# The output product of pairs 1 to 3 as seven half-size products, and a written-out order for every engine

## The chip, the cores and the metric

The kernel runs on one core of one Trainium2 chip. The metric is the device time of one execution in microseconds, given as the median of the timed runs; lower is better.

## The reference, cut to what matters

Attention in two stages (32 packed queries `p` attend to `k`, `v`; then the 576 queries `q` attend to the packed result) gives `x` of 4608 tokens by 512. A feed-forward layer follows, and it is most of the work:

```python
p_packed = sm_attn(p, k, v)
out = sm_attn(q, p_packed, p_packed)          # 8 batches, 8 heads, 576 queries, 64 wide
x = out.transpose(0, 2, 1, 3).reshape(4608, 512)
h = x @ w_in                                   # 512 -> 2048
g = 0.5 * h * (1.0 + erf(h / sqrt(2)))
return (g @ w_out).astype(np.float32)          # 2048 -> 512
```

Everything is float32.

## The kernel before, in words

The eight batches are worked in four pairs (`pr` 0 to 3), and the 2048 hidden columns in four blocks of 512 (`f`), so there are 16 units `u = 4 * pr + f`. In pair 0 the weights come from DRAM, are decoded to full words on ACT, DVE and POOL (`decode`), and are kept in a DRAM scratch (`keep`); pairs 1 to 3 load them from there, one 512 KB piece at a time (`w<-ws`, L1774).

Float32 accuracy is had from three matmuls in the rounded type float32r: each operand is split into a high part (a cast on ACT) and a low part (operand minus high part, on DVE), and high x high, high x low and low x high are added up in PSUM.

A unit has eight hidden steps (`hidden_steps`, L1936 to L1974): a step gives 128 hidden columns of one batch, 12 matmuls of 288 columns on L1957 into a `wide` tile (two buffers of two PSUM banks). `gelu` (L1976) takes it through Gelu on ACT (L1979), then splits it: 512 of the 576 tokens on ACT (L1986) and DVE (L1988) into `g`, the other 64 on POOL (L1999, L2000) into `t4`, the tile of the tokens at the edge of both batches. Each hidden step is followed by an output step (`output_steps`, L2034): four token tiles of 128, three matmuls of 512 columns each (`three`, L2008: L2009, L2010, L2011), with a token tile of `g` as the weights and a row block of `w_out` as the moving operand. Four output steps fill a PSUM tile; `edge_output` does the same for the edge tile. `finish` (L2111) copies the PSUM tile into `acc` at `f = 0` (L2115, ACT), adds it at later `f` (L2120, DVE), and writes the rows out at `f = 3`. The very last edge tile is done in two halves of 256 columns (`last_rows`, L2083; L2101, L2102).

The order of the instructions on each engine is fixed at build time. `Order` plays the kernel as a set of tasks against modelled costs (the second argument of each `Op`) and at each turn of an engine issues the first ready operation by a priority, made of the tables `SLACK`, `EARLY` and `SOONER` and of `PATIENCE`. The attention of pair `pr + 1` runs on all engines beside the units of pair `pr`. All DMAs are issued by SP's queue, in order.

## Time and profile before

| what | value |
|---|---|
| timed runs | 721.12 us median of 3 (720.46 to 721.38) |
| profiled execution | span 718.7 us, first to last instruction; what lies around the span isn't in the page, and the timed runs are 1.8 to 2.7 us above it |
| granted TensorE clock | mean 1.000 of full |
| busy | PE 99%, weight loads 82%, DVE 54%, ACT 49%, POOL 23% |
| DMA | 106.76 MB, 149 GB/s mean |

A PE instruction's time in the profile is from its start to its modelled end, and the next one starts before that end; so a rate is read from the starts of a run of matmuls, and not from their durations.

### The profile page before, as it was taken

To read this page: it belongs to the slowest core of one execution; us is meant where nothing else is said; L and a number is where in the kernel's file an instruction comes from. 1 tells how busy PE (TensorE), PEld (TensorE's weight loads), DVE (VectorE), ACT (ScalarE), POOL (GpSimd) and SP (SyncE) were. 2 spreads that over 40 slices of the span, in tenths; PEclk is the share of its full clock that TensorE was granted. 3 is DMA by queue.
4 is the path that set the end of the run, shared out by engine and by line. 5 is a ranking of instruction groups with operands and counts; after the bars stand their busy time and mean duration, and the time that the engine had idled before them with its cause. 6 is when DMAs were issued, how large, how long until landed. Compare 5 with 4: busy or idle time off the path is not lost.

```text
span 718.7 us, 13236 instructions
## 1 busy us (share of the span) xinstructions
PE 712.2 (99%) x5278; PEld 586.0 (82%) x5278; DVE 389.5 (54%) x613; ACT 350.9 (49%) x589; POOL 162.1 (23%) x318
## 2 busy tenths in 40 slices
...
GB/s 320 355 212 222 210 260 184 225 203 298 135 102 156 179 180 188 8 225 18 163 81 146 228 172 209 9 110 75 131 158 42 222 60 88 60 29 88 1 118 73
DMA packets 156797, 106.76 MB, mean 149 GB/s; under 512 B 124353, under 2 KB 132801, under 8 KB 156737
## 3 DMA queue, kind: packets, MB, share of 16 engines
...
## 4 chain that ended last, share of the span: by engine, by line
PE 94%; DMA 2%; DVE 2%; ACT 1%; SPq 0%; issue 0%; ACTq 0%
PE h L1957 26%; PE o L2009 17%; PE o L2011 16%; PE o L2010 16%; PE wps L1891 4%; PE h L1948 2%; PE s L1351 2%; PE o_edge L2009 2%; PE o_edge L2011 2%; PE o_edge L2010 2%; PE pp L1544 1%; DMA wraw<-in_moe_w_in_dram 1%; PE idle L1930 1%; DMA v<-in_v_dram 1%; PE e1Tm L1457 1%; DVE wp L1907 1%
## 5 line engine op out<-in xcount | busy, mean ns | idle before, releaser
L1957 PEld LDWEIGHTS h<-a2T,wp 128*128 128x128 f32 x1440 | 202.9, 188 | 9.8 <-PE h L1957 0.5
L1957 PE MATMUL h<-a2T,wp 128*128 128x288 f32 x1440 | 210.2, 295 | 0.3 <-DVE wp L1907 0.3
L2009 PE MATMUL o<-w,g 128*128 128x512 f32 x508 | 204.1, 402 | 0.0
L2011 PE MATMUL o<-w,g 128*128 128x512 f32 x508 | 198.5, 391 | 0.2 <-DVE g L1988 0.2
L2010 PE MATMUL o<-w,g 128*128 128x512 f32 x508 | 198.4, 391 | 0.0
L1988 DVE TENSOR_TENSOR g<-graw,g 128x512 fp32r<-128x512 f32 x128 | 93.3, 731 | 182.8 <-ACT g L1986 179.9
L1979 ACT ACTIVATE graw<-h 128x576 f32<-128x576 f32 x128 | 83.3, 652 | 200.2 <-PE h L1957 151.4
L1999 POOL CAST t<-graw 128x64 fp32r<-128x64 f32 x128 | 39.8, 311 | 466.7 <-ACT graw L1979 283.5
L2009 PEld LDWEIGHTS o<-w,g 128*128 128x128 f32 x508 | 95.4, 188 | 37.0 <-issue 21.5
L2011 PEld LDWEIGHTS o<-w,g 128*128 128x128 f32 x508 | 95.4, 188 | 21.8 <-DVE g L1988 0.6
L2010 PEld LDWEIGHTS o<-w,g 128*128 128x128 f32 x508 | 95.4, 188 | 14.9
L1986 ACT CAST g<-graw 128x512 fp32r<-128x512 f32 x128 | 79.4, 621 | 56.2 <-PE o L2011 53.7
L2120 DVE TENSOR_TENSOR acc<-o,acc 128x512 f32<-128x512 f32 x96 | 63.5, 684 | 36.2 <-PE o L2011 36.1
L1907 DVE TENSOR_TENSOR wp<-wps,wp 128x1024 fp32r<-128x1024 f32 x30 | 35.9, 1218 | 29.6 <-ACT wp L1902 29.5
L2000 POOL TENSOR_TENSOR t<-graw,t 128x64 fp32r<-128x64 f32 x128 | 46.9, 366 | 10.2
L1902 ACT CAST wp<-wps 128x1024 fp32r<-128x1024 f32 x30 | 29.6, 1016 | 30.5 <-PE wps L1891 30.4
L1891 PE MATMUL wps<-w,pp 64*32 64x512 f32 (+1 forms) x528 | 32.3, 575 | 0.0
L1861 POOL TENSOR_TENSOR wt<-wt 128x512 int32<-128x512 int32 x16 | 21.8, 1361 | 34.6 <-DVE wt L1832 30.0
L1853 POOL TENSOR_TENSOR w<-wt 128x512 int32<-128x512 int32 x16 | 22.5, 1412 | 24.4 <-DVE wt L1832 16.5
L2009 PE MATMUL o_edge<-w,t 128*128 128x512 f32 (+1 forms) x68 | 25.8, 379 | 0.0
L2010 PE MATMUL o_edge<-w,t 128*128 128x512 f32 (+1 forms) x68 | 25.7, 377 | 0.0
L2011 PE MATMUL o_edge<-w,t 128*128 128x512 f32 (+1 forms) x68 | 25.7, 377 | 0.0
...
## 6 DMA issues: line engine op xcount, KB each, us to landing
w<-ws SPq DMA_DIRECT2D x72, 512.0 KB, 4.9
ws<-w SPq DMA_DIRECT2D x24, 512.0 KB, 4.6
v<-in_v_dram SPq DMA_DIRECT2D x16, 512.0 KB, 6.4
wraws<-in_moe_w_out_dram SPq DMA_DIRECT2D x16, 512.0 KB, 5.3
k<-in_k_dram SPq DMA_DIRECT2D x48, 144.0 KB, 4.9
q<-in_q_dram SPq DMA_DIRECT2D x48, 144.0 KB, 5.1
...
wraws<-in_moe_w_in_dram SPq DMA_DIRECT2D x12, 512.0 KB, 4.3
```

Source lines behind the costliest of these rows:

```text
L1891: nc.tensor.matmul(t[r0:r0 + 32, hh, :m], lhsT=pp[b][rows, hh, r0:r0 + 32], rhs=wi[u, hh][rows, g, cols], start=True, stop=True)
L1907: yield Op(DVE, 1.2, step, lambda: nc.vector.tensor_tensor(lo, x, hi.bitcast(F32), ALU.subtract))
L1957: nc.tensor.matmul(t[:, half, :HALF], lhsT=w[:, wpart, ch, fc], rhs=a2T[b, ch][:, apart, half * HALF:(half + 1) * HALF], start=ch == 0 and ...
L1979: lambda raw: nc.scalar.activation(raw.rearrange("p (a n) -> p a n", a=2), t[:, :, :HALF], AF.Gelu),
L1986: g = yield Op(ACT, 0.52, lead, lambda g: nc.scalar.copy(g[:, 0], main), [(gts, f"g_{n}")])
L1988: DVE, 0.6, lead, lambda: nc.vector.tensor_tensor(g[:, 1], main, g[:, 0].bitcast(F32), ALU.subtract),
L1999: nc.gpsimd.tensor_copy(dst[:, 0], side)
L2000: nc.gpsimd.tensor_tensor(dst[:, 1], side, dst[:, 0].bitcast(F32), ALU.subtract)
L2009: nc.tensor.matmul(t, lhsT=g[0], rhs=w[:, 0], start=first, stop=False)
L2010: nc.tensor.matmul(t, lhsT=g[0], rhs=w[:, 1], start=False, stop=False)
L2011: nc.tensor.matmul(t, lhsT=g[1], rhs=w[:, 0], start=False, stop=last)
L2120: yield Op(DVE, 0.6, n, lambda: nc.vector.tensor_tensor(a, x, a, ALU.add))
```

## The change

Pair 0 keeps the old output product. In pairs 1 to 3 a unit's Gelu output of 512 hidden columns by two batches of 576 tokens is seen as a 2 by 2 block matrix (rows: the two batches; columns: the two halves of the hidden block) and `w_out`'s block as a 2 by 2 matrix of 256 by 256 pieces. The eight block products become seven (Strassen's scheme in Winograd's form), and the output is made transposed: 128 output columns on the partitions, the 576 tokens of a batch along the free axis.

- Weights. In pair 0 the decoded `w_out` goes to DRAM a second time as full words (`whole`), a block is read back, four differences are made on POOL (`mixed_weights`), split on ACT and DVE (`mixed_weight`) and stored; the three unmixed operands are stored from the split pieces (`keep_blocks`). In pairs 1 to 3 a unit loads seven pieces of 512 KB (`load_mixed`) in place of four.
- Operands. `gelu` writes the whole 576 tokens into one of the blocks `a11`, `a12`, `a21`, `a22`; the split of `g` and the POOL work of the edge tile are gone in these pairs. `sums` makes four sums and differences on POOL, 128 by 1152 each. `splits` and `low` split the seven operands: a cast on ACT and a subtraction on DVE, 128 by 1152 each (in the last unit two of the subtractions are on POOL).
- Products. `mixed_steps`: for each of the seven, two halves `h` of 12 matmuls of 288 columns; the weights are a slice of every second column of the piece, `w[:, :, q * 256 + h:q * 256 + 256:2]`. There are two PSUM tiles of two banks (`mps`, one for each half) in place of the four single banks. The products `a11`, `s2`, `s3`, `s1` follow each other in one open PSUM group (`CHAIN`): the sum is copied out behind each of them and goes on growing, so that a half's product waits for the `evicted` of the same half of the product before it.
- Results. `evict` copies (ACT, at `f = 0`) or adds (DVE) 128 by 576 to one of five sums `mac`. At a pair's end `results` combines them with three POOL operations of 128 by 1152, in-place, and the adds of `s4` into `c12` wait for these (`mixed_up`); `turned_back` transposes 32 by 32 on DVE, and `result` writes each quarter with four DMAs in runs of 256 bytes.
- Order. `TURNS` lists for each engine every operation in the order of its issue, in place of the priorities; it covers all four pairs. SBUF tiles are laid out by hand in two tensors, where later tiles take the room of earlier ones (`Slots`).

```diff
+MIXED = ("a22", "a11", "s2", "s3", "s1", "s4", "a12")
+NM = len(MIXED)
+LAST_LOW = (2, 4)
+CHAIN = ("a11", "s2", "s3", "s1")
+INTO = {"a22": "m4", "a11": "c11", "s2": "c12", "s3": "u3", "s1": "c22", "s4": "c12", "a12": "c11"}
...
+TURNS = {
+    PE: (
+        "53 62 64 56 63 57 80 83 61 81 68 82 100 101 112 119 118 84 96 97 93 92 94 71 138 73 153 72 114 108 133 "
...
+        ready, turns, n = self.ready[engine], self.turns, self.turn[engine]
+        key = next(iter(ready), None) if self.dry else turns[engine][n] if n < len(turns[engine]) else None
+        if key in ready and self.issuable(ready[key][0]):
+            op, go_on, begin = ready.pop(key)
+            self.turn[engine] += 1
...
+    middle = lay(0, ("x", 7, X), ("v", 2, 4 * 20 * D), ("sm", 4, ROWS), ("wi", 2, BOTH))
+    end = max(
+        lay(middle, ("sm_more", 2, ROWS), ("wi_more", 1, BOTH), ("wt", 3, BOTH), ("graw", 3, ROWS), ("acc", 9, EITHER)),
+        lay(middle, ("x_more", 3, X), ("mac", 7, X)))
...
+    end = max(
+        lay(ROUNDED, ("g", 3, BOTH), ("t4", 4, 4 * 2 * P), ("wo", 6, BOTH)),
+        lay(ROUNDED, ("wm", 4, BOTH), ("op", 3, 2 * X)))
+    rounded = const.tile([P, (end - ROUNDED) // 4], F32R, name="rounded")
+    pairs = [ps_o.tile([P, 2, 512], F32, name=f"oh_{i}") for i in range(2)]
...
+        psum_o = of_banks(
+            [(i, i + 1, lambda i=i: pairs[i // 2][:, i % 2]) for i in range(4)], [P, 512], (None, (0, 1, 2, 3)))
+        mps = of_banks([(2 * i, 2 * i + 2, lambda i=i: pairs[i][:]) for i in range(2)], [P, 2, 512], (None, (0, 1)), rank=1)
...
+        blocks_of_w = slots("x", [P, 2, FB], F32, (2 * NF, (5, 6)), rank=0.5)
+        bigs = slots("x x_more", [P, 2, S], F32, (None, (2, 7, 8, 9, 5, 6)), rank=1, free=True)
+        ops = slots("op", [P, 2, 2, S], F32R, (None, (0, 1, 2)), rank=1)
+        wms = slots("wm", [P, 2, FB], F32R, (None, (0, 1, 2, 3)), rank=1)
+        macs = slots("mac", [P, 2, S], F32, (None, tuple(range(7))), rank=1, free=True)
...
+        def keep_blocks(f, i, src, step):
+            big_f, q = divmod(i - 2, 2)
+            mine = (("a11", 0),) if big_f == 0 else (("a12", 0), ("s4", 1))
+
+            def fn():
+                for name, v in mine:
+                    d = mixed_w[f, MIXED.index(name)][:, :, q * 256:q * 256 + 256]
+                    nc.sync.dma_start(d, src.bitcast(F32)[:, :, v * 256:v * 256 + 256])
+
+            yield Op(DMA, (len(mine), 400e3 * len(mine)), step, fn)
+            fire(stored[f, i])
+            for name, _ in mine:
+                fire(mixed_stored[f, MIXED.index(name)])
+
+        def mixed_weights(f):
+
+
+            yield whole_stored[f]
+            got = []
+            for big_f in range(2):
+                def fetch(t, big_f=big_f):
+                    for side in range(2):
+                        nc.sync.dma_start(
+                            t[:, side].rearrange("p (q x) -> p q x", q=2),
+                            whole[f][:, 2 * big_f:2 * big_f + 2, side * 256:side * 256 + 256])
...
+                got.append((yield Op(DMA, (2, 800e3), 0, fetch, [(blocks_of_w, f"bw_{f}_{big_f}")])))
+            (b11, b12), (b21, b22) = ((t[:, 0], t[:, 1]) for t in got)
+            t1, t3, t2, t4_ = b11, b12, b22, b21
+            left = Event(4)
+            for x, y, z in ((t1, b12, b11), (t3, b22, b12), (t2, b22, t1), (t4_, t2, b21)):
+                yield Op(
+                    POOL, 1.2, 0, lambda x=x, y=y, z=z: nc.gpsimd.tensor_tensor(x, y, z, ALU.subtract))
+            yield [mixed_weight(f, MIXED.index(name), x) for name, x in (("a22", t4_), ("s2", t2), ("s3", t3), ("s1", t1))]
+            for t in got:
+                blocks_of_w.give(t)
+            fire(blocks_done)
+
+        def mixed_weight(f, m, x):
+            both = yield Op(
+                ACT, 0.62, 0, lambda d: nc.scalar.copy(d[:, 0], x), [(mws, f"mw_{f}_{m}")])
+            yield Op(
+                DVE, 0.74, 0,
+                lambda: nc.vector.tensor_tensor(both[:, 1], x, both[:, 0].bitcast(F32), ALU.subtract),
+                port=True)
+            yield Op(DMA, (1, 524e3), 0, lambda: nc.sync.dma_start(mixed_w[f, m], both.bitcast(F32)))
+            fire(mixed_stored[f, m])
+            mws.give(both)
...
         def gelu(n, u, j, c, t, lead):
+            if u >= NF:
+                name = f"a{2 - j}{c // 2 + 1}"
+                x = big[u, name] = yield from one(bigs, f"big_{u}_{name}", ACT, lead)
+                yield Op(
+                    ACT, 0.68, lead,
+                    lambda: nc.scalar.activation(
+                        x[:, c % 2].rearrange("p (a n) -> p a n", a=2), t[:, :, :HALF], AF.Gelu), table="gelu")
+                wide.give(t)
+                fire(value[u, name])
...
+            psum_o.closed = True
+            start(mixed_steps(), "products")
+
+        def sums(u):
+            def of(name):
+                return big[u, name]
+
+            def done(name):
+                return split_done[u, MIXED.index(name)]
+
+            def put(x, y, z, op):
+                return Op(POOL, 2.4, 0, lambda: nc.gpsimd.tensor_tensor(of(x), of(y), of(z), op))
+
+            yield value[u, "a21"]
+            yield value[u, "a22"]
+            big[u, "s1"] = yield Op(
+                POOL, 2.4, 0, lambda s: nc.gpsimd.tensor_tensor(s, of("a21"), of("a22"), ALU.add),
+                [(bigs, f"big_{u}_s1")])
+            fire(value[u, "s1"])
+            yield value[u, "a11"]
+            yield put("a21", "a11", "a21", ALU.subtract)
+            fire(value[u, "s3"])
+            yield done("a22")
+            bigs.give(of("a22"))
+            fire(freed[u, "a22"])
+            yield done("a11")
+            yield put("a11", "s1", "a11", ALU.subtract)
+            fire(value[u, "s2"])
+            yield value[u, "a12"]
+            yield done("s2")
+            yield put("a11", "a12", "a11", ALU.subtract)
+            fire(value[u, "s4"])
+            for name, x in (("s3", "a21"), ("s1", "s1"), ("s4", "a11"), ("a12", "a12")):
+                yield done(name)
+                bigs.give(of(x))
+                fire(freed[u, x])
+
+        def splits(u):
+            where = {"s2": "a11", "s3": "a21", "s4": "a11"}
+            for m, name in enumerate(MIXED):
+                yield value[u, name]
+                x = big[u, where.get(name, name)]
+                o = op[u, m] = yield Op(ACT, 1.17, 0, lambda o: nc.scalar.copy(o[:, 0], x), [(ops, f"op_{u}_{m}")])
+                start(low(u, m, o, x))
+
+        def low(u, m, o, x):
+            engine, cost = (POOL, 2.4) if u == NU - 1 and m in LAST_LOW else (DVE, 1.43)
+            yield Op(
+                engine, cost, 0, lambda: on(engine).tensor_tensor(o[:, 1], x, o[:, 0].bitcast(F32), ALU.subtract), port=True)
+            fire(split_done[u, m])
...
+        def mixed_steps():
+            for u in range(NF, NU):
+                chain = {}
+                for m, name in enumerate(MIXED):
+                    for h in range(2):
+                        for t8 in range(8):
+                            if -(-t8 * 2 * NM // 8) == 2 * m + h:
+                                n = 8 * u + t8
+                                fire(begun[n])
...
+                    yield wm_ready[u, m]
+                    o, w = op[u, m], wm[u, m]
+                    first = name not in CHAIN[1:]
+                    for h in range(2):
+                        def product(*new, h=h):
+                            t = new[0] if new else chain[h]
+                            for q in range(2):
+                                x = w[:, :, q * 256 + h:q * 256 + 256:2]
+                                for wpart, parts in ((0, (0, 1)), (1, (0,))):
+                                    for part in parts:
+                                        for half in range(2):
+                                            nc.tensor.matmul(
+                                                t[:, half, :HALF], lhsT=x[:, wpart],
+                                                rhs=o[:, part, q, half * HALF:(half + 1) * HALF],
+                                                start=first and q == 0 and wpart == 0 and part == 0,
+                                                stop=q == 1 and wpart == 1, skip_group_check=not first)
+
+                        if not first:
+                            yield evicted[(*divmod(u * NM + m - 1, NM), h)]
+                        got = yield Op(PE, 1.59, 0, product, [(mps, f"m_{u}_{m}_{h}")] if first else [])
+                        if first:
+                            chain[h] = got
+                        start(evict(u, m, h, chain[h]))
+                    ops.give(o)
+                    wms.give(w)
+                    fire(multiplied[u, m])
+
+        def evict(u, m, h, t):
+            pr, f = divmod(u, NF)
+            x, name = t[:, :, :HALF], INTO[MIXED[m]]
+
+            def to():
+                return mac[pr, name][:, h].rearrange("p (a n) -> p a n", a=2)
+
+            if f == 0 and m < 5:
+                mac[pr, name] = yield from one(macs, f"mac_{pr}_{name}", ACT, 0)
+                yield Op(ACT, 0.66, 0, lambda: nc.scalar.copy(to(), x))
+            else:
+                if m >= 5:
+                    yield added[u, name, h]
+                if f == NF - 1 and name == "c12" and m >= 5:
+                    yield mixed_up[pr]
+                yield Op(DVE, 0.75, 0, lambda: nc.vector.tensor_tensor(to(), x, to(), ALU.add))
+            if MIXED[m] not in CHAIN[:-1]:
+                mps.give(t)
+            fire(evicted[u, m, h])
+            if m < 5:
+                fire(added[u, name, h])
+            if f == NF - 1:
+                fire(total[pr, m])
...
+        def results(pr):
+            engine, cost = POOL, 2.4
+
+            def of(name):
+                return mac[pr, name]
+
+            def combine(x, y, z, op):
+                return Op(engine, cost, 0, lambda: on(engine).tensor_tensor(of(x), of(y), of(z), op), port=True)
+
+            def totals(*names):
+                for name in names:
+                    yield total[pr, MIXED.index(name)]
+
+            yield from totals("a22", "s3")
+            yield combine("m4", "u3", "m4", ALU.subtract)
+            start(result(pr, 0, 0, "m4"))
+            yield from totals("s2")
+            yield combine("c12", "c12", "u3", ALU.subtract)
+            macs.give(of("u3"))
+            yield from totals("s1")
+            yield combine("c12", "c12", "c22", ALU.add)
+            fire(mixed_up[pr])
+            start(result(pr, 0, 1, "c22"))
+            yield from totals("s4")
+            start(result(pr, 1, 1, "c12"))
+            yield from totals("a12")
+            start(result(pr, 1, 0, "c11"))
+
+        def result(pr, j, v, name):
+            src = mac[pr, name]
+            y = yield Op(DVE, 0, 0, lambda t: None, [(macs, f"res_{pr}_{name}")])
+            z = y.rearrange("p h s -> p (h s)").rearrange("p (b c n) -> p b c n", b=NB32, n=2)
+            yield [turned_back(z, src, h) for h in range(2)]
+            macs.give(src)
+            r0 = (2 * pr + j) * S
+
+            def fn():
+                for a in range(4):
+                    rows = out[r0:r0 + S, v * 256 + a * 64:v * 256 + a * 64 + 64].rearrange("(b t) x -> t b x", t=32)
+                    nc.sync.dma_start(rows, z[32 * a:32 * a + 32].rearrange("p b c n -> p b (c n)"))
+
+            yield Op(DMA, (4, 800e3), 0, fn)
+            macs.give(y)
+            fire(ended[pr])
+
+        def turned_back(z, src, h):
+            yield Op(
+                DVE, 0.78, 0,
+                lambda: nc.vector.transpose(z[:, :, :, h], src[:, h].rearrange("p (b c) -> p b c", b=NB32)))
 
         def edge_output(u, n):
```

## Rows read from the trace of the kernel before

**Rows 1.** The page: busy time by engine, shares of the chain.

```profile
PE 712.2 (99%) x5278; PEld 586.0 (82%) x5278; DVE 389.5 (54%) x613; ACT 350.9 (49%) x589; POOL 162.1 (23%) x318
PE 94%; DMA 2%; DVE 2%; ACT 1%; SPq 0%; issue 0%; ACTq 0%
```

**Rows 2.** Windows by pair: us; busy PE, PEld, DVE, ACT, POOL; clock, DMA.

```profile
0.00:220.00 220.00, 216.79 (x1850) 172.70 (x1851) 167.40 (x276) 147.57 (x261) 101.59 (x126) 1.00 0.79 224
...
390.00:562.00 172.00, 172.00 (x1273) 142.03 (x1272) 85.18 (x128) 75.41 (x125) 21.21 (x64) 1.00 0.57 131
562.00:716.00 154.00, 153.44 (x900) 130.82 (x898) 51.70 (x77) 51.15 (x78) 19.87 (x64) 1.00 0.23 78
```

**Rows 3.** PE timeline, first and last of 22 (start us, us, what).

```profile
601.09 0.40 PE L2009 MATMUL o<-w,g 128*128 128x512 f32 x1
...
605.86 0.39 PE L2009 MATMUL o<-w,g 128*128 128x512 f32 x1
```

**Rows 4.** The chain, a hidden step near its end (start us, us, what).

```profile
701.20 1.58 PE h L1957 x12
```

**Rows 5.** PE timeline of the end, first and last of 24.

```profile
712.41 0.28 PE L2009 MATMUL o_edge<-w,t 128*128 128x256 f32 x1
...
715.16 0.28 PE L2011 MATMUL o_edge<-w,t 128*128 128x256 f32 x1
```

**Rows 6.** Weight loads of three lines (count, ns min/median/max, starts).

```profile
L1457 PEld LDWEIGHTS e1Tm<-ident,e x60: 195/207/216, 15.4 to 530.5; 128*128 128x128 f32 x60
L1273 PEld LDWEIGHTS qm<-ident,q x36: 138/140/143, 19.4 to 39.7; 128*128 128x128 f32 x36
L1957 PEld LDWEIGHTS h<-a2T,wp x1440: 186/188/192, 84.2 to 706.7; 128*128 128x128 f32 x180
```

**Rows 7.** L1457's matmuls: durations, and four in the PE timeline.

```profile
L1457 PE MATMUL e1Tm<-ident,e x60: 270/283/385, 15.5 to 530.6; 128*128 128x128 f32 x60
32.48 0.64 PE L1457 MATMUL e1Tm<-ident,e 128*128 128x128 f32 x4
```

**Rows 8.** DVE groups of pair 2 (count, busy us, mean ns, idle before).

```profile
L1988 DVE TENSOR_TENSOR g<-graw,g 128x512 fp32r<-128x512 f32 x34 | 23.5, 690 | 50.2 <-ACT g L1986 50.0
L2120 DVE TENSOR_TENSOR acc<-o,acc 128x512 f32<-128x512 f32 x25 | 16.8, 688 | 5.2 <-PE o L2011 5.2
L1907 DVE TENSOR_TENSOR wp<-wps,wp 128x1024 fp32r<-128x1024 f32 x8 | 9.6, 1219 | 7.9 <-ACT wp L1902 7.8
L1665 DVE STREAM_TRANSPOSE a<-e 128x576 f32<-128x576 f32 x4 | 3.1, 772 | 0.1
```

**Rows 9.** A group of ACT over the span.

```profile
L1902 ACT CAST wp<-wps 128x1024 fp32r<-128x1024 f32 x30 | 29.6, 1016 | 30.5 <-PE wps L1891 30.4
```

**Rows 10.** L1634's durations, and the timeline of POOL and DVE around 50 us.

```profile
L1634 POOL TENSOR_TENSOR e<-e,mx x3: 1158/1159/1612, 31.2 to 47.6; 128x576 f32<-128x576 f32 x3
L1634 DVE TENSOR_TENSOR e<-e,mx x13: 747/749/1834, 50.3 to 557.4; 128x576 f32<-128x576 f32 x13
50.21 1.29 POOL L1867 TENSOR_TENSOR w<-wt,w 128x512 fp32r<-128x512 f32 x1
50.27 1.83 DVE L1634 TENSOR_TENSOR e<-e,mx 128x576 f32<-128x576 f32 x1
```

**Rows 11.** Timeline behind the last matmul.

```profile
715.48 0.42 DVE L2101 TENSOR_TENSOR acc<-o_edge,acc 128x256 f32<-128x256 f32 x1 [1.01 <-PE o_edge L2011]
715.93 0.33 SPq L2102 DMA_DIRECT2D out_dram<-acc  x1
```

**Rows 12.** DMA issues (count, KB, us to landing), and three in the timeline.

```profile
k<-in_k_dram SPq DMA_DIRECT2D x48, 144.0 KB, 4.9
out_dram<-acc SPq DMA_DIRECT2D x36, 64.0 KB, 1.7
w<-ws SPq DMA_DIRECT2D x72, 512.0 KB, 4.9
78.64 3.38 SPq L1240 DMA_DIRECT2D q<-in_q_dram  x3
```

1074 lines of the change are left out of this document (259 added, 815 removed), and 100 rows, old and new, of the table TURNS.

## The prediction

> **What bounds the kernel now.** I began with the page: PE is busy 99% of the span and holds 94% of the chain that ended last [rows 1]. A busy share alone doesn't say that PE works at its rate, since a matmul's recorded time is longer than its turn; so I then cut the span by the ends of the pairs, read off the last output writes (near 220, 390, 562 and 716 us). In pairs 2 and 3 PE has no idle time worth a sum (172.0 of 172 and 153.4 of 154 us), at a granted clock of 1.00, which is the 2.4 GHz level, while DVE has 85 and 52 us of work, ACT 75 and 51, POOL some 20 [rows 2]; pair 1 looks like pair 2. There time is the number of matmuls by their spacing, and an engine beside PE matters only when it is late. In pair 0 DVE has 167 us in 220 and ACT 148 [rows 2].
>
> The spacing comes from the timeline. In the output product 21 steps of 512 columns take 4.77 us, 227.1 ns each [rows 3]; a hidden step of 12 matmuls of 288 columns takes 1.58 us on the chain, 131.7 ns each [rows 4]; 23 steps of 256 columns take 2.75 us, 119.6 ns each [rows 5]. That is 0.420 ns a column and some 11 to 12 ns for each instruction, so smaller matmuls pay more for the same columns.
>
> **The change, part by part.** *Output product.* Before, a unit has 8 steps and the edge, 36 tiles by 3 matmuls: 108 x 0.2271 = 24.5 us. After, it has 14 halves of 12 matmuls of 288 columns. If these go at the hidden step's pace, 14 x 1.58 = 22.1 us. The columns fall by an eighth, the time by a tenth: 2.41 us a unit, **28.9 us** over 12 units. Their number is 12 x 168 = 2016, so 14 ns more for each would eat it all.
>
> *Weights of every second column.* This is the one thing in those 2016 matmuls that the hidden step doesn't have. The trace has strided weights in one place: L1457 transposes slices with a stride of two (pair 0) or four. Its loads take 207 ns, those of L1273, contiguous and else alike, 140 [rows 6]: 67 ns more. The hidden step's loads take 188 [rows 6] and vanish behind 131.7 ns spacing; they vanish behind 119.6 too [rows 5]. From above: if the 67 ns come on top of a load that already fills 119.6, the spacing is 186.6, 55 ns more, 2016 x 0.055 = 111 us. From below: nothing, since a load can't be slower than hidden and still cost less. Which is nearer? Four L1457 transposes take 0.64 us with the last one's 0.283, so they follow each other at (0.64 - 0.283) / 3 = 119 ns, each with its strided load [rows 7]. A strided load stream of 128 columns of 4 bytes thus passes in 119 ns, under 131.7. I take nothing, and keep 55 ns as a rival.
>
> The Trainium skill (SBUF — State Buffer, in the section on the DMA port swizzle) says that two hits to a 16-byte line are enough for full speed, which a stride of two float32 has: by it the weights cost nothing and the sum is the one below. The trace agrees only in part: L1457's loads are 67 ns slower with a stride of two just as with four [rows 6]. With that added in full the sum would be 111 us higher.
>
> *Evictions.* Two PSUM tiles serve all 14 halves, so the half after next waits for each eviction, in the open group through `evicted` and elsewhere for the tile. DVE's add of 512 columns takes 688 ns, 1024 columns 1219 [rows 8]: 1.04 ns a column, so 576 take 0.755 and 1152 take 1.35 us. The handovers at the end of the span are some 0.05 us: the last matmul ends at 715.16 + 0.28 = 715.44 [rows 5], DVE starts at 715.48 [rows 11]. So an eviction is done 0.86 us after its half, and the next need is 1.58 us after it: 0.72 us to spare, more where a hidden step stands between.
>
> *DVE, POOL, ACT.* In pairs 1 and 2 DVE loses 32 splits of 0.690 and 27 adds of 0.688 (40.7 us, [rows 8]) and gains 28 low parts of 1.35 (37.8), 46 evictions of 0.755 (34.7) and 8 transposes of 0.772 (6.2, [rows 8]): 85 - 41 + 79 = 123 us of about 162, 76%. In pair 3: 52 - 41 + 79 - 3 = 87 of 144. POOL loses its edge tiles, nearly all of its 20 us, and gets 19 operations a pair of 1152 columns, by 1.159 for 576 [rows 10] 2.32 us each, 44 us. ACT's casts of 1152, scaled from 1.016 for 1024 [rows 9], take 1.14 us, 28 of them 32 us; even if nothing were removed, it has 107 of 162. None reaches PE. But they queue: a DVE subtraction from SBUF that met a POOL operation (50.21 to 51.50) took 1.83 us where 0.749 is usual [rows 10], as if it had waited for POOL's end. An eviction behind a low part that has just begun is done after 0.05 + 1.35 + 0.755 + 0.05 = 2.2 us, and PE waits 0.62; behind one that POOL holds up it waits up to 2.3 more. The written order can put hidden steps there (8 beside 14 halves), so not each meets it. Bounds: none of the 168 halves, or one in three, 56 x 0.62 = 35 us. I take one in 16, **6.5 us**, as in the old trace PE lost next to nothing with DVE at half load.
>
> *End.* Behind the last old matmul come an add (0.42) and one DMA; the span ends 718.7 - 715.44 = 3.3 us after it [rows 11]. Behind the new one: eviction 0.81, transpose 0.82, 0.05, then four issues on SP's queue. Three issues in a row took 3.38 us with the queues full [rows 12], the last one of the span 0.33 [rows 11], so the fourth starts 1.0 to 3.4 us later; it lands after 1.7 us (64 KB in long runs) to 4.9 us (144 KB in runs of 128 bytes; here 256) [rows 12]. That is 4.4 to 10 us, or 1.1 to 6.7 more; I take **4**. `mixed_up` adds to it in pair 3, where nothing else is left for PE: behind `s1` come an eviction (0.86), POOL (2.32 + 0.05) and the add of `s4` (0.81), 4.0 us, while the two halves of `s4` cover 3.16: **0.9**.
>
> *Hand-over from pair 0 to 1.* The new tiles lie where `acc`, `graw` and `wt` lay, so first sums wait for pair 0's rows to be written (landing 1.7 us, [rows 12]); units 3 and 4 overlap, so 0 to 3 us, I take **1**.
>
> *Costed at nothing.* Mixed weights: 16 differences, casts and low parts in pair 0, some 11 us of DVE in 220 where 53 were idle [rows 2]; the cover is PE's own work, and without it they cost those 11. Seven loads of 512 KB a unit for four: PE uses one in 3.16 us, four buffers ask 12.6 us ahead, and one lands in 4.9 [rows 12]; DMA share is 0.57 [rows 2]. Each engine's written order replaces another fixed order; its pair 0 may be a few us better or worse, which no row tells.
>
> **Sum.** 718.7 - 28.9 + 6.5 + 4 + 0.9 + 1 = 702.2 us of span. The timed median stands 2.4 above the profiled span, so 704.6: **705 us**.
>
> **The rivals.**
> *Evictions late.* DVE at 76% with a gate at every half is a queue. For it: no gate of this kind before, and POOL's operations are twice as long as any seen. Against: 0.72 us to spare and hidden steps between. From one half in five (34 x 0.62 = 21 us) it gives 719; at one in three 733. This is the way to no change, and to slower from one in four (42 x 0.62 = 26 us, 724).
> *Strided weights show.* Slower, by one mechanism: it decides from 14 ns a matmul. For it the 67 ns of [rows 6]; against it the 119 ns of [rows 7]. At 35 ns, 705 + 71 = 776; in full, 816.
> *Nothing is late.* No stall and the short end: 718.7 - 28.9 + 1.1 + 0.9 + 2.4 = 694, less if the new order of pair 0 is better.
> *Pair 0 or the hand-over lags* by tens of us, as the new areas wait for old tiles and the order is fixed: 735 and up.
>
> **How the numbers follow.** Forecast (694 to 717) 0.65; late evictions (717 to 735) 0.15, of which 0.05 still faster, 0.03 the same, 0.07 slower; strided weights 0.13; below 694 0.04; a lag in pair 0 0.03. A difference of 0.2% is about what a measurement here can tell from none: faster 0.65 + 0.05 + 0.04 = 0.74, same 0.03, slower 0.07 + 0.13 + 0.03 = 0.23. The range 693 to 732 takes in the forecast and nearly all of the late evictions, and leaves out the weights, a lag and little else.
>
> **What would show it.** Right: the mixed matmuls 131 to 133 ns apart, 1.58 us a half on the chain, though their loads may be recorded at up to 255 ns; PE's idle time before the halves under 10 us in all, put down to DVE evictions; DVE at some 123 us in pairs 1 and 2; POOL operations of 2.3 us; pairs 1 and 2 at 163 to 166 us and pair 3 some 145; an end of 6 to 8 us behind the last matmul. Wrong: halves longer than 1.7 us (the weights), DVE ahead of PE on the chain (evictions), or an end of pair 0 well past 220 us.

## The result, and the profile after

| | median | lowest to highest | ratio to before, 95% interval |
|---|---|---|---|
| before | 721.09 us | 720.46 to 721.38 | |
| changed | 728.62 us | 725.6 to 730.59 | 1.0100 (1.0076 to 1.0124) |

The kernel is 1% slower where 2% faster was forecast. The profiled execution is the shortest of the changed kernel: 723.8 us of span, 5.1 above the 718.7 of before. The median lies 3 us above this execution, and what those 3 us are its profile can't show. The page of the changed kernel, beside [rows 1] (busy times, the chain, the costliest groups; L1809 are the mixed products, L1734 the sums, L1771 the low parts, L1840 the evictions, L1765 the casts, L1856 the sums of the results):

```profile
PE 695.9 (96%) x6003; PEld 613.5 (85%) x6003; DVE 518.5 (72%) x695; ACT 392.0 (54%) x596; POOL 290.8 (40%) x201
...
PE 82%; DVE 6%; DMA 5%; ACT 3%; issue 2%; SPq 1%; DVEq 0%; ACTq 0%
...
L1809 PE MATMUL oh<-rounded 128*128 128x288 f32 x2016 | 293.5, 299 | 7.4 <-issue 3.2
L1809 PEld LDWEIGHTS oh<-rounded 128*128 128x128 f32 x2016 | 276.0, 197 | 27.7 <-issue 12.2
...
L1734 POOL TENSOR_TENSOR memory<-memory 128x1152 f32<-128x1152 f32 x36 | 103.5, 2875 | 138.9 <-ACT memory L1650 94.0
L1840 DVE TENSOR_TENSOR memory<-oh,memory 128x576 f32<-128x576 f32 x138 | 102.3, 747 | 68.4 <-PE oh L1809 53.2
L1771 DVE TENSOR_TENSOR rounded<-memory,rounded 128x1152 fp32r<-128x1152 f32 x82 | 124.1, 1523 | 26.3 <-ACT rounded L1765 26.2
L1765 ACT CAST rounded<-memory 128x1152 fp32r<-128x1152 f32 x84 | 96.6, 1158 | 51.2 <-PE oh L1809 24.6
...
L1856 POOL TENSOR_TENSOR memory<-memory 128x1152 f32<-128x1152 f32 x9 | 27.9, 3113 | 17.5 <-DVE memory L1840 17.3
```

The cast, the eviction and the weight load stand near their estimates; the two-operand work does not: the low part took 1.52 us where 1.35 was estimated, the sums 2.88 and 3.11 where 2.32 was. PE holds 82% of the chain, 94% before, and 5% of it is now DMA. Cut into stretches, beside [rows 2] (columns: busy time of PE, weight loads, DVE, ACT, POOL, granted clock, DMA share, GB/s):

```profile
0.00:220.00 220.00, 211.95 (x1815) 165.08 (x1815) 165.43 (x272) 144.43 (x261) 115.11 (x138) 1.00 0.85 246
220.00:390.00 170.00, 165.31 (x1492) 148.30 (x1476) 129.75 (x165) 97.84 (x137) 49.79 (x20) 1.00 0.78 204
390.00:562.00 172.00, 171.41 (x1582) 158.34 (x1583) 128.24 (x161) 90.86 (x127) 61.61 (x22) 1.00 0.73 178
562.00:712.00 150.00, 146.76 (x1130) 141.50 (x1130) 91.57 (x94) 58.87 (x71) 64.32 (x22) 0.99 0.44 129
```

PE idles 8.05, 4.69, 0.59 and 3.24 us; before it idled 3.2 us up to 220 and none from 220 to 712. So the pair in the middle went about as told, and the loss lies in the first two pairs and at the end.

The ends of pairs alone mislead here, because the changed order does more hidden steps ahead. The view of stretches for the hidden step's line alone (L1957 before, L1625 after; x12 to a step), cut at the last output product of pair 1 and of pair 2, shows it, before and then after:

```profile
0.00:393.90 393.90, 103.42 (x708) 99.70 (x708) 1.00 0.70 184
393.90:564.40 170.50, 56.14 (x384) 54.02 (x384) 1.00 0.58 133
564.40:718.70 154.30, 50.63 (x348) 49.17 (x348) 1.00 0.22 74
```

```profile
0.00:412.40 412.40, 112.18 (x768) 105.76 (x769) 1.00 0.80 222
412.40:572.30 159.90, 52.42 (x360) 48.87 (x360) 1.00 0.76 180
572.30:723.80 151.50, 45.31 (x312) 42.45 (x312) 0.96 0.47 133
```

That is 59, 32 and 29 steps of 12 before and 64, 30 and 26 after (the plain ones of pair 0, 64 matmuls on either side, are on a line of their own). The products of the packed weights (L1891 before, L1542 after; 16 matmuls to a group, 1.0 us from start to start) shift too: 320, 128 and 96 matmuls before, 336, 144 and 64 after. At 1.58 us a step [rows 4] and 1.0 us a group, like is compared with like:

| stretch | time | steps shifted | groups shifted | net | the prediction's terms |
|---|---|---|---|---|---|
| pairs 0 and 1 | 393.9 to 412.4: +18.5 | 5 more: -7.9 | 1 more: -1.0 | **+9.6** | -9.6 + 2.2 + 1 = -6.4 |
| pair 2 | 170.5 to 159.9: -10.6 | 2 fewer: +3.2 | 1 more: -1.0 | **-8.4** | -9.6 + 2.2 = -7.4 |
| pair 3, to the last product's end | 151.0 to 140.2: -10.8 | 3 fewer: +4.7 | 2 fewer: +2.0 | **-4.1** | -9.6 + 2.2 + 0.9 = -6.5 |
| behind it | 3.3 to 11.3 | | | **+8.0** | +4 |

(28.9 us over three pairs is 9.6, 6.5 is 2.2. The last product ends at 704.39 + 8.13 = 712.52 us, below.) Against the prediction, 16 us were lost in pairs 0 and 1, 2.4 in pair 3 and 4 at the end; pair 2 came out 1 better.

**Where pair 0 falls behind.** The kernel fills PE's waits in the first 55 us with matmuls on a tile of zeros (fillers; L1930 before, L1596 after), which count as busy. The first 60 us, all of PE and then the fillers alone, before and then after:

```profile
0.00:60.00 60.00, 57.32 (x671) 43.47 (x672) 44.01 (x90) 43.32 (x85) 29.31 (x34) 1.00 0.96 283
0.00:60.00 60.00, 20.23 (x150) 14.99 (x150) 1.00 0.96 283
```

```profile
0.00:60.00 60.00, 54.76 (x662) 40.29 (x663) 40.58 (x83) 39.54 (x79) 27.82 (x28) 1.00 0.89 276
0.00:60.00 60.00, 24.45 (x167) 16.90 (x167) 1.00 0.89 276
```

Without fillers PE has been busy for some 37.1 us by then before and for 30.3 after; by 220 us it is 216.79 - 20.23 = 196.6 and 211.95 - 24.45 = 187.5. So of the 9 us that PE is behind at 220 us, 7 are there after 60.

**Where pair 1 waits.** The chain of the changed kernel from 289 to 321 us:

```profile
289.74 2.99 SPq L824
292.78 3.58 SPq L824
296.40 3.88 DMA memory<-in_k_dram
...
301.70 0.65 DVE memory L1514
...
304.31 4.67 DMA wx<-memory
309.06 0.62 ACT memory L1511
...
311.38 1.78 PE h L1625 x12
313.16 6.02 DMA rounded<-wx
...
319.32 1.83 PE oh L1809 x12
```

L824 are the `k` loads of pair 2. Two issues take 2.99 and 3.58 us on SP, while the DMA share is above 1 (1.03 to 1.26 from 290 to 296 us). A mixed weight's low part (L1514) stands in DVE's list behind the `k` transposes, its store (`wx<-memory`) behind `q` loads, the cast of the next mixed weight (L1511) behind the store, and three loads of mixed weights (`rounded<-wx`) behind all of them: a product waits until 319.32. SP itself waits for nothing here: from 287.84 to 315.45 us its issues follow each other with gaps of at most 0.15 us. The windows of 296 to 316 us, before and after:

```profile
296.00:316.00 20.00, 20.00 (x165) 15.08 (x171) 10.58 (x14) 6.30 (x13) 2.43 (x9) 1.00 0.58 98
```

```profile
296.00:316.00 20.00, 17.28 (x156) 14.79 (x155) 13.63 (x19) 9.38 (x17) 0.00 (x0) 1.00 1.06 204
```

**The end.** The timeline of PE, DVE, POOL and SP from 698 us (start, duration, then in brackets the idle time before):

```profile
698.43 3.41 PE L1809 MATMUL oh<-rounded 128*128 128x288 f32 x24 [0.29 <-issue]
704.39 8.13 PE L1809 MATMUL oh<-rounded 128*128 128x288 f32 x48 [2.55 <-issue]
...
699.41 3.55 DVE L1771 TENSOR_TENSOR rounded<-memory,rounded 128x1152 fp32r<-128x1152 f32 x1 [0.41 <-ACT rounded L1765]
702.88 1.41 DVE L1840 TENSOR_TENSOR memory<-oh,memory 128x576 f32<-128x576 f32 x2
...
708.21 0.76 DVE L1840 TENSOR_TENSOR memory<-oh,memory 128x576 f32<-128x576 f32 x1 [2.57 <-POOL memory L1856]
...
699.07 9.10 POOL L1856 TENSOR_TENSOR memory<-memory 128x1152 f32<-128x1152 f32 x3 [2.63 <-DVE memory L1840]
...
705.71 14.48 SPq L1888 DMA_DIRECT2D out_dram<-memory  x16
```

The low part begins 0.34 us after POOL's first sum and takes 3.55 us; the evictions behind it in DVE's list are late, PE idles 2.55 us, and 24 matmuls that took 3.4 us are followed by 48 in 8.13, because the clock fell to the 1.2 GHz level (windows of the same kernel, granted clock third from the right):

```profile
704.00:706.00 2.00, 1.61 (x7) 1.64 (x8) 1.63 (x3) 0.00 (x0) 1.92 (x2) 0.64 0.00 0
706.00:708.00 2.00, 2.00 (x11) 2.00 (x10) 0.00 (x0) 0.00 (x0) 2.00 (x1) 0.51 0.63 107
...
716.00:718.00 2.00, 0.00 (x0) 0.00 (x0) 0.00 (x0) 0.00 (x0) 0.00 (x0) 0.50 1.01 208
```

From 716 us nothing but the results' transfers is left, at a DMA share of 1.01 and 208 GB/s at first.

### The profile page after: what moved, and what is told of

The parts are those of the page before. It is cut to its first block, busy times and chain, and to the rows that moved or that the text cites. A ratio compares the mean times of both kernels' runs of the same rounds, so it can differ in the third digit from the quotient of the medians.

```text
span 723.8 us, 14815 instructions
## 1 busy us (share of the span) xinstructions
PE 695.9 (96%) x6003; PEld 613.5 (85%) x6003; DVE 518.5 (72%) x695; ACT 392.0 (54%) x596; POOL 290.8 (40%) x201
## 4 chain that ended last, share of the span: by engine, by line
PE 82%; DVE 6%; DMA 5%; ACT 3%; issue 2%; SPq 1%; DVEq 0%; ACTq 0%
PE oh L1809 35%; PE h L1625 23%; PE wps L1542 4%; PE oh L1687 3%; PE oh L1689 3%; PE oh L1688 3%; PE s L937 2%; DMA rounded<-wx 2%; PE h L1616 1%; PE pp L1128 1%; PE oh L1596 1%; SPq L824 1%; DMA wraws<-in_moe_w_out_dram 1%; DVE rounded L1666 1%; DVE memory L1927 1%
## 5 line engine op out<-in xcount | busy, mean ns | idle before, releaser
L1809 PE MATMUL oh<-rounded 128*128 128x288 f32 x2016 | 293.5, 299 | 7.4 <-issue 3.2
L1809 PEld LDWEIGHTS oh<-rounded 128*128 128x128 f32 x2016 | 276.0, 197 | 27.7 <-issue 12.2
L1625 PE MATMUL h<-a2T,wp 128*128 128x288 f32 x1440 | 209.9, 295 | 1.1 <-ACT memory L991 0.6
L1625 PEld LDWEIGHTS h<-a2T,wp 128*128 128x128 f32 x1440 | 197.1, 188 | 5.4 <-ACT memory L991 1.3
L1734 POOL TENSOR_TENSOR memory<-memory 128x1152 f32<-128x1152 f32 x36 | 103.5, 2875 | 138.9 <-ACT memory L1650 94.0
L1840 DVE TENSOR_TENSOR memory<-oh,memory 128x576 f32<-128x576 f32 x138 | 102.3, 747 | 68.4 <-PE oh L1809 53.2
L1771 DVE TENSOR_TENSOR rounded<-memory,rounded 128x1152 fp32r<-128x1152 f32 x82 | 124.1, 1523 | 26.3 <-ACT rounded L1765 26.2
L1765 ACT CAST rounded<-memory 128x1152 fp32r<-128x1152 f32 x84 | 96.6, 1158 | 51.2 <-PE oh L1809 24.6
L1650 ACT ACTIVATE memory<-h 128x576 f32<-128x576 f32 x96 | 61.6, 651 | 96.8 <-PE h L1625 91.4
L1739 POOL TENSOR_TENSOR memory<-memory 128x1152 f32<-128x1152 f32 x12 | 32.8, 2734 | 150.5 <-ACT memory L1650 150.5
L1687 PE MATMUL oh<-rounded 128*128 128x512 f32 x128 | 53.3, 416 | 1.8 <-DVE memory L1927 1.8
L1689 PE MATMUL oh<-rounded 128*128 128x512 f32 x128 | 50.3, 393 | 0.1
L1688 PE MATMUL oh<-rounded 128*128 128x512 f32 x128 | 50.1, 391 | 0.0
L1457 POOL TENSOR_TENSOR memory<-memory 128x512 int32<-128x512 int32 x16 | 21.5, 1346 | 40.7 <-DVE memory L1429 26.3
L1657 ACT ACTIVATE memory<-h 128x576 f32<-128x576 f32 x32 | 20.8, 651 | 31.1 <-PE h L1625 19.9
L1687 PEld LDWEIGHTS oh<-rounded 128*128 128x128 f32 x128 | 24.1, 188 | 14.5 <-issue 7.3
L1542 PE MATMUL wps<-memory,pp 64*32 64x512 f32 (+1 forms) x544 | 35.5, 575 | 0.0
L1856 POOL TENSOR_TENSOR memory<-memory 128x1152 f32<-128x1152 f32 x9 | 27.9, 3113 | 17.5 <-DVE memory L1840 17.3
L846 DVE STREAM_TRANSPOSE memory<-memory 128x1152 f32<-128x1152 f32 x24 | 32.9, 1369 | 2.0 <-DMA memory<-in_k_dram 1.8
```

The source lines that it names most:

```text
L1542: nc.tensor.matmul(t[r0:r0 + 32, hh, :m], lhsT=pp[b][rows, hh, r0:r0 + 32], rhs=wi[u, hh][rows, g, cols], start=True, stop=True)
L1625: nc.tensor.matmul(t[:, half, :HALF], lhsT=w[:, wpart, ch, fc], rhs=a2T[b, ch][:, apart, half * HALF:(half + 1) * HALF], start=ch == 0 and ...
L1650: lambda: nc.scalar.activation(x[:, c % 2].rearrange("p (a n) -> p a n", a=2), t[:, :, :HALF], AF.Gelu), table="gelu")
L1687: nc.tensor.matmul(t, lhsT=g[0], rhs=w[:, 0], start=first, stop=False)
L1688: nc.tensor.matmul(t, lhsT=g[0], rhs=w[:, 1], start=False, stop=False)
L1689: nc.tensor.matmul(t, lhsT=g[1], rhs=w[:, 0], start=False, stop=last)
```

## The experiments

The kernel before ran beside each group at 720.99 to 721.14 us. Intervals are lowest to highest of the runs.

**Strided weights.** `e1_contig` takes neighbouring columns.

```diff
-x = w[:, :, q * 256 + h:q * 256 + 256:2]
+x = w[:, :, q * 256 + h * 128:q * 256 + h * 128 + 128]
```

> The weights of a mixed product are 128 neighbouring columns in place of every second one; the columns of the output come out in another order. If strided weights cost what the transposes' loads suggest, the 2016 matmuls get faster by tens of ns each and the kernel by 20 us or more (below 708). If they are hidden, as the changed kernel's own trace suggests with 1.59 to 1.60 us for 12 matmuls against 1.58 to 1.59 in the hidden step, at most 1 ns a matmul, 2 us in all, is there to be had: 724 to 730.

727.08 us (726.2 to 728.03), ratio 1.0084 (1.0067 to 1.0101) against 1.0100 (1.0076 to 1.0124): no difference. The strided loads are hidden.

**The making of the mixed weights.** `e2_nomix` leaves it out, with its transfers.

```diff
-                yield Op(DMA, (1, 262e3), step, lambda: nc.sync.dma_start(whole[f][:, i - 2], full.bitcast(F32)))
...
-            yield whole_stored[f]
...
-            yield mixed_stored[u % NF, m]
+            m0 = m if MIXED[m] in ("a11", "s4", "a12") else MIXED.index("a11")
+            yield mixed_stored[u % NF, m0]
```

> Leaves out the making of the four mixed weights: no second store of the decoded weights, no reading back, no differences, splits and stores; pairs 1 to 3 load the stored piece of a11 in their place, as many bytes as before, so these products are not those of the scheme. All else keeps its order. Theory A (the mixed weights in pair 0 and their DMAs in pair 1 fill ACT's, DVE's and SP's queues, and PE waits behind them): pair 0 ends 4 to 8 us sooner and pair 1 takes 5 to 9 us less, 712 to 718 in all. Theory B (DVE's low parts held up by POOL's sums in pairs 1 to 3): at most 3 us less, 724 to 728.

719.77 us (718.77 to 721.54), ratio 0.9981 (0.9971 to 0.9990): 8.9 us less than the changed kernel, the largest lump found. In its trace the last matmul of pair 1's products starts at 405.7 us instead of 412.3, so 6.6 us are there by the end of pair 1; they are there at the end of its second unit (318.0 for 324.6 us), where only 2.2 were at the end of its first (276.5 for 278.7).

**The length of POOL's and DVE's operations.** `e3_pool_small` lets the sums work on 32 of the 576 tokens of a batch, `e4_low_small` the low parts (and multiplies the high part in their place, so that PE keeps its work).

```diff
-tensor_tensor(of(x), of(y), of(z), op)
+tensor_tensor(of(x)[:, :, :32], of(y)[:, :, :32], of(z)[:, :, :32], op)
```

```diff
-tensor_tensor(o[:, 1], x, o[:, 0].bitcast(F32), ALU.subtract)
+tensor_tensor(o[:, 1, :, :32], x[:, :, :32], o[:, 0, :, :32].bitcast(F32), ALU.subtract)
```

> Three of the four sums of a unit and the three combinations of a pair work on 32 of 576 tokens, so POOL is nearly free in pairs 1 to 3; operands and results are not those of the scheme in the other tokens. Theory B: DVE's low parts fall from 1.52 us towards 1.35, the stall of 2.55 us near the end goes, PE's lost time in pairs 1 to 3 falls by 8 us or more: 715 to 720. Theory A: only the end gains, 3 to 4 us: 723 to 726.

> The low parts of the seven operands are made for 32 of 576 tokens, and the high part is multiplied in their place, so DVE loses some 38 us a pair and PE keeps its work; the sums lose accuracy. Theory B (DVE as the queue that PE waits for): PE's lost time in pairs 1 to 3 falls by 10 us or more: 712 to 719. Theory A: at most 4 us, mostly at the end: 722 to 728.

723.91 us (722.05 to 725.4) and 724.11 us (722.68 to 725.5), ratios 1.0041 (1.0026 to 1.0055) and 1.0045 (1.0029 to 1.0062): 4.7 and 4.5 us. In the trace of `e3_pool_small` pairs 1 and 2 end as in the changed kernel (last matmul at 412.4 and 572.0 us for 412.3 and 572.1); only the last unit is shorter. In that of `e4_low_small` they end no sooner either (413.0 and 572.5 us). So in the middle the longer operations of POOL and the low parts on DVE cost nothing: evictions were not the trouble.

**The start, a little order, the issue of results.** `e5_start` puts the numbers of the first 44 us of `TURNS` in the sequence of the kernel before. `e6_order` moves three transfers in the list. `e7_tail` lets ACT issue every second result. `e8_two` has both of the last two.

```diff
+queue = nc.scalar if pr == NP - 1 and a % 2 else nc.sync
-nc.sync.dma_start(rows, z[32 * a:32 * a + 32].rearrange("p b c n -> p b (c n)"))
+queue.dma_start(rows, z[32 * a:32 * a + 32].rearrange("p b c n -> p b (c n)"))
```

> The changed kernel, with the order of the first 44 us of every engine's list and of the transfers put back as in the kernel before; what follows keeps its order, and no work is added or left out. In the changed kernel TensorE is busy for 211.95 us of the first 220, in the kernel before for 216.79, and the first hidden product starts at 49.5 us instead of 41.5. Theory (the new order of the start costs time by itself, beside the mixed weights): the first hidden product comes back to about 42 us, TensorE's busy time in the first 220 us rises by 2 to 3 us, and the whole is 2 to 3 us below the changed kernel, 725 to 727 us. Rival (the new start only does the same work in another sequence, since the second unit's hidden product starts at 85.3 us against 84.5 before): no change, 728 to 729 us, or up to 4 us more, because the old start now meets the added stores of decoded weights.

> The changed kernel, with three transfers moved ahead in the one list of transfers near 298 us: the store of the third mixed weight of the last block of weights goes ahead of the first q load of pair 2, the store of its fourth and the load of one mixed weight go ahead of the second q load. Nothing else moves. Theory (the products of pair 1 wait at 306 to 319 us because the k and q loads stand ahead of these small transfers in SyncE's queue): the wait of 5.7 us of ScalarE at 303 to 309 us and that of TensorE ahead of 319.3 us get shorter by 3 to 4 us, and the whole falls by 3 to 4 us to about 725 us. Rival (the q loads are as urgent as the stores, so that the scores of pair 2 are late in their place): the waits move to 320 to 350 us and the whole stays at 728 to 729 us.

> The changed kernel, with every second transfer of a result in the last pair issued by ScalarE instead of SyncE; ScalarE is idle there. After the last product (712.5 us) the changed kernel takes 11.3 us, and the last eight issues of results take some 5 us in SyncE's queue one after the other. Theory (the end is as long as the queue of issues): the last issue comes 2 to 3 us earlier and the whole falls by 2 to 3 us, to 725.5 to 726.5 us. Rival (the end is set by the transfers themselves, 3.4 us from issue to landing with many small pieces): less than 1 us.

> The changed kernel with the edits of the two runs before together: three transfers moved ahead near 298 us, and every second result of the last pair issued by ScalarE. Theory (the two losses lie one behind the other on the same chain): the gains add up, 5 to 7 us below the changed kernel, 722 to 724 us. Rival (one of them is taken back by what is late next): no more than the larger of the two alone, 725 us or more.

727.42 (725.28 to 729.86), 729.7 (724.02 to 732.14), 726.73 (725.13 to 731.9) and 726.26 us (724.95 to 727.22). None is clear of the changed kernel, and the rivals had it: with the old start PE was busy for 209.16 us of the first 220, not 214; with the three transfers moved, the second unit of pair 1 ended 4.4 us earlier (320.2 for 324.6 us, start of its last matmul) and pair 1 only 1.0 earlier, as another load of a mixed weight then came 2.2 us late at 338.5; with two queues for the results the span still ended 11 us behind the last product.

**Work or transfers?** `e9_traffic` keeps all transfers of the making and drops its work. `e10_nostore` keeps the work and drops the 16 stores.

```diff
-yield [mixed_weight(f, MIXED.index(name), x) for name, x in (("a22", t4_), ("s2", t2), ("s3", t3), ("s1", t1))]
+yield [store(f, MIXED.index(name), t) for name, t in (("a22", got[0]), ("s2", got[1]), ("s3", got[0]), ("s1", got[1]))]
```

```diff
-            yield Op(DMA, (1, 524e3), 0, lambda: nc.sync.dma_start(mixed_w[f, m], both.bitcast(F32)))
             fire(mixed_stored[f, m])
             mws.give(both)
```

> The changed kernel with all transfers of the mixed weights (decoded weights out, blocks in, mixed weights out, 16.8 MB) but none of the work on them: the blocks that were fetched are stored as they are, so that GpSimd's 16 differences, ScalarE's 16 roundings and VectorE's 16 low parts are left out, and the mixed weights hold other numbers. Leaving out work and transfers together gave 719.8 us against 728.6. Theory 1 (the transfers cost: they fill the queue and the DMA engines, on which the k and q loads of pair 2 and the mixed weights then wait): 727 to 729 us, the waits at 300 to 320 us stay. Theory 2 (the work costs: it stands in the engines' lists, in order, and waits there for transfers): 720 to 722 us.

> The changed kernel with the mixed weights worked out as before but not stored (16 stores of 512 KB left out); units then load one of the three that are plain blocks in their place, as many bytes as before. Theory 1 (all transfers cost alike): half of the 16.8 MB is gone, so about half of the 8.9 us: 724 to 725 us. Theory 3 (the chain of a mixed weight through its store: ScalarE waits for the buffer that the store before it frees, 5.7 us at 303 to 309 us, and holds up what is behind it): 720 to 722 us. By theory 2 of the run beside it: 727 to 729 us, since all of the work stays.

725.54 us (722.11 to 727.51), ratio 1.0059 (1.0039 to 1.0078), and 721.05 us (720.23 to 722.65), ratio 1.0000 (0.9992 to 1.0009). The work is worth 3.1 us of the 8.9, at the edge of the noise, the stores 7.6; the two overlap. Theories 1 and 2 both miss the time of the first, but the waits that theory 1 expected are in its trace; for the second the time is theory 3's. PE's waits for mixed weights from 270 to 420 us (in all, times, longest), in `e9_traffic` and then in `e10_nostore`:

```profile
PE oh L1820 <- DMA rounded<-wx: 6.2, 2, 5.1
```

```profile
PE oh L1824 <- DMA rounded<-wx: 1.1, 1, 1.1
```

So without the work the waits stay, and without the stores all but 1.1 us of them go. In the window of `e10_nostore` that answers to the two above, PE has no idle time:

```profile
296.00:316.00 20.00, 20.00 (x182) 18.21 (x181) 16.41 (x28) 14.12 (x23) 1.56 (x1) 1.00 0.90 170
```

**How do the stores cost?** `e13_buffers` takes away the wait for the one buffer (theory 3), `e14_early` adds the order, `e17_queue` changes the queue alone.

```diff
-mws = slots("wt", [P, 2, FB], F32R, (4 * NF, (2,)))
+mws = slots("wt mw_more", [P, 2, FB], F32R, (4 * NF - 4, (2,)), (4, (3, 4)))
```

```diff
-nc.sync.dma_start(mixed_w[f, m], both.bitcast(F32))
+nc.gpsimd.dma_start(mixed_w[f, m], both.bitcast(F32))
```

> The changed kernel, with two buffers instead of one for the four mixed weights of the last block of weights, which are made from 264 to 313 us; all work, transfers and lists stay. Theory (the wait for the one buffer costs): ScalarE no longer waits 5.7 us at 303 to 309 us, TensorE's waits at 311 to 319 us fall by 2 to 3 us, and the whole is 2 to 3 us below the changed kernel, 725 to 726.5 us. Rival (the transfers cost, by their bytes and their place in the queue): the waits for mixed weights and k loads stay, 727.5 to 729 us.

> The kernel of the run before, with the rounding and low part of the third and fourth mixed weight of the last block moved ahead of the k transposes that wait for their loads, and their stores and one load of a mixed weight moved ahead of the q loads of pair 2. Theory (order): the second and third unit of pair 1 end 4 to 5 us earlier than in the changed kernel and keep it: 723 to 725 us. Rival (bytes: what is moved ahead pushes the q loads back, as in the run that moved three transfers): the gain of the second unit is given back by the third, no better than the buffers alone.

> The changed kernel with the 16 stores of the mixed weights issued by GpSimd instead of SyncE; all else stays. Theory (the place in SyncE's queue: a store waits there for VectorE's low part, and the loads behind it with it): 723 to 725 us, the waits for mixed weights near 313 to 319 us go. Rival (bytes: the DMA engines are busy without a gap near 300 us, whoever issues): 727 to 729 us, and the k loads' issues stay at 2 us each.

729.36 (726.99 to 730.3), 725.62 (721.79 to 728.42) and 731.66 us (727.76 to 735.1). The first sinks theory 3: in its trace ACT waits no more near 303 us (L1512 runs at 304.13), and PE waits 5.4 us in pair 1 for `rounded<-wx`, up to 3.8 at once, where it waited 2.1 for these and 2.1 for DVE. The order on top of it gives some 3 us (ratio 1.0055, 1.0037 to 1.0072); its trace doesn't show where, as the second unit of pair 1 ends 1.9 us sooner (322.7 for 324.6 us) and the third no sooner (368.9 for 368.8). Another queue gives nothing: PE still waits 2.3 us for mixed weights in pair 1, and the DMA share of 296 to 316 us is 1.16. But POOL now waits up to 10.3 us for DVE ahead of a store, so that this run is no clean test of the queue's worth in time. What it does show is what an issue depends on. Four `k` issues of pair 2 on SP, in the changed kernel, in `e17_queue` and in `e10_nostore`:

```profile
289.21 8.07 SPq L824 DMA_DIRECT2D memory<-in_k_dram  x4
```

```profile
293.09 8.08 SPq L824 DMA_DIRECT2D memory<-in_k_dram  x4
```

```profile
283.42 5.87 SPq L839 DMA_DIRECT2D memory<-in_k_dram  x4
```

They are shorter where the stores are gone, and not where another queue sends them. From the first of these issues to the three loads of mixed weights it is 23.95 us in the changed kernel (289.21 to 313.16), 24.38 in `e17_queue` (293.09 to 317.47) and 20.80 in `e10_nostore` (283.42 to 304.22). So the place of the stores in SP's queue isn't the cause; the slower issues are.

**The end.** `e11_pieces` writes the last pair's results in runs of 512 bytes. `e12_warm` keeps PE busy in its wait. `e15_last` puts two of the three last sums on DVE, lets the results go in the order in which they are then ready and ACT issue every second one, all on top of `e14_early`; `e16_last_buffers` is that without the moved order.

```diff
+r1, c1 = r0 + HALF * (a % 2), v * 256 + 128 * (a // 2)
+rows = out[r1:r1 + HALF, c1:c1 + 128].rearrange("(b t) x -> t b x", t=32)
```

```diff
+if (u, m, h) == (NU - 1, 5, 0) and not order.dry:
+    idle = wide.next("warm")
+    for _ in range(20):
+        nc.tensor.matmul(bank(idle)[:, :256], lhsT=still[:, :P], rhs=still, start=True, stop=True)
```

```diff
+engine, cost = DVE, 1.43
 yield from totals("s3", "s2")
 yield combine("c12", "c12", "u3", ALU.subtract)
 yield from totals("s1")
 yield combine("c12", "c12", "c22", ALU.add)
```

> The changed kernel, with the results of the last pair written in pieces of 512 bytes instead of 256: the same transfers from the same places, the same bytes into the same blocks of the output, but to other rows and columns there. From 716 to 722 us the DMA engines are busy for 0.95 or more of the time and move some 200 GB/s; in the kernel before 64 KB results of whole rows moved at 326 to 381 GB/s. Theory (the end is set by the pieces of 256 bytes): the last result lands 3 to 4 us earlier after the last product, 7.5 to 8.5 us instead of 11.3, and the whole is 725 to 726 us. Rival (the end is set by the transposes and the issues that precede): under 1 us.

> The changed kernel with 20 matmuls of 256 columns on a tile of zeros put ahead of the sixth product of the last unit, where TensorE waits for 2.55 us (701.84 to 704.39 us) and then runs at half its clock until 708. They take about 2.2 us, so they fit into the wait. Theory (the wait is what takes the clock): the granted clock stays 1.00 from 700 to 712 us, the last 48 products take 6.4 us instead of 8.1, and the last product ends 1.7 us earlier; the whole falls by 1 to 1.7 us at most, since transfers follow. Rival (the clock falls whatever TensorE does in the wait, or GpSimd's sums set the end, since they hold up the results): no change.

> The kernel of the run before, and in the last unit of the last pair two of the three sums of the results on VectorE, the third on GpSimd behind them, results in the order in which they are then ready, and every second transfer of a result issued by ScalarE. Theory (GpSimd's three sums of 3 us each, one behind the other, set the end of the products, and they lengthen VectorE's low part to 3.6 us): the last product ends 3 to 4 us earlier against the start of the unit, the whole falls by 2 to 3 us against the run before. Rival (the end is set by 2.36 MB of results in pieces of 256 bytes and by VectorE's transposes): under 1 us.

> The changed kernel with two buffers for the last block's mixed weights and the last unit as in the run before, without the moved order near 290 us. If the order gives nothing or costs, this is the fastest of the four: 722 to 724 us by the theories of the buffers and of the last unit, 727 to 728 us by their rivals. Faster than the kernel before (721.1 us) by neither.

725.47 us (724.46 to 726.63; ratio 1.0064, 1.0051 to 1.0077), 726.76 (725.19 to 729.55), 725.32 (722.75 to 727.62) and 727.68 (726.31 to 731.44). With longer runs the span ends 722.8 - 713.88 = 8.9 us behind the last product, 2.4 less; its window of 716 to 718 us:

```profile
716.00:718.00 2.00, 0.00 (x0) 0.00 (x0) 0.55 (x1) 0.00 (x0) 0.00 (x0) 0.92 0.94 244
```

Of `e12_warm`, PE's timeline:

```profile
703.35 2.36 PE L1807 MATMUL warm<-still 128*128 128x256 bf16 x20
706.03 3.42 PE L1814 MATMUL oh<-rounded 128*128 128x288 f32 x24 [0.32 <-issue]
710.73 3.42 PE L1814 MATMUL oh<-rounded 128*128 128x288 f32 x24 [1.28 <-issue]
```

The clock stays, 24 matmuls take 3.42 us again, and the next 24 then wait 1.28 us: the add of `s4` waits for POOL's last sum (until 709.88 us). So the fall of the clock was covered by that wait. In `e15_last` the clock stays and two of the sums are off POOL; the last product ends 139.7 us after pair 2's last matmul starts (569.3 to 708.95), where the changed kernel takes 140.4 (572.1 to 712.52), and the span ends 151.9 us after it, where the changed kernel takes 151.7. The low part still takes 3.56 us there, beside the one sum that is left on POOL, and PE still waits 1.91 and 0.77 us, so the run doesn't free the products of POOL. The products' 0.7 us don't reach the end: from 708 us the DMA share is 0.94 to 1.06, so it is likely that the transfers of the results set it. No complete version beat the kernel before; `e15_last`, run once more as `e18_last_queue`, gave 724.59 us (722.78 to 729.03).

## Why the prediction was wrong

- **PE's own time: right.** 12 mixed matmuls take 1.58 to 1.60 us on the chain (1.79 behind a packed product), where 1.58 was taken; 132 to 133 ns from one to the next. Pair 2, the undisturbed one, gained 8.4 us net, where the matmuls alone were to give 9.6.
- **Strided weights: right.** Their loads took 197 ns against 188 for the contiguous ones of the hidden step, and `e1_contig` changes nothing. The 67 ns of [rows 6] did not carry over.
- **Evictions: size right, cost too high.** 747 ns for 755. The 6.5 us for one late eviction in 16 didn't come: from 412.4 to 572.3 us PE idles 0.13 us in all, and `e3_pool_small` shows that POOL, whose holding of DVE was the reason for the term, costs nothing before the last unit. That pair 2 is still within 1 us of its forecast is partly luck: the late evictions are missing, and the matmuls gave less. DVE had 130 and 128 us of work in pairs 1 and 2 where 123 were taken, and was not the bound.
- **"Costed at nothing": the step that failed.** The cover named for the mixed weights was idle time of DVE in pair 0, and for the seven loads a DMA share of 0.57. The price of the making was not DVE's 11 us: leaving it out gave 8.9 of the 24.0 us by which the median missed, and 7.6 came with the stores alone. The prediction counted the loads and left out that the making's own transfers (16.8 MB of the 33.7 that came on top of 106.76) run past 300 us, into the stretch in which pair 2's `k` and `q` are loaded; a mean share over 170 us hid that. [rows 12] had the parts: `k` loads of 144 KB that land after 4.9 us, three `q` issues in 3.38 us, all on one queue. That the stores cost PE these waits is shown by `e10_nostore` beside `e9_traffic`. The way is longer issues on SP (8.07 us for four `k` loads, 8.08 with the stores on another queue, 5.87 without them). That an issue is long because the DMA engines are full is argued, not shown.
- **"Its pair 0 may be a few us better or worse": put at nothing too, and too small.** Of the 16 us missed in pairs 0 and 1, 6.6 went with the making by the end of pair 1 (412.3 to 405.7). Some 9 stay open. Most of them arise in the first 60 us, where PE, fillers left out, is 7 us behind: 30.3 us of work for 37.1. It is no better without the making (55.25 - 25.31 = 29.9 us in `e2_nomix`) and hardly better with the old order of the list's first 44 us (53.34 - 21.70 = 31.6 in `e5_start`). The cause of this is open; the new layout of the tiles is a rival that no run tested. 2.1 of PE's 4.8 us of added idle time up to 220 us went with the making's work.
- **Hand-over: not seen.** From 220 to 278.7 us, the end of pair 1's first unit, PE idles 0.33 us where 1 was taken.
- **End: a wait of this kind was foreseen, its size was not.** 8.0 us where 4 was taken, above the 6.7 that the bounds allowed. The issue was priced by one queue's turn; in `e7_tail` a second queue still leaves 11.0 us behind the last product, in `e11_pieces` longer runs save 2.4 us of 11.3 (the other traces have 10.6 to 12.3). 2.36 MB of results leave behind 705 us, at 174 to 208 GB/s where the DMA share is above 0.9; before, 256 KB results in rows of 2 KB left at 326 to 381. The Trainium skill (DMA: Bandwidth & Descriptors, section Specifications) names 512 bytes as the least transfer for full rate; the trace agrees in direction, with 208 GB/s at 256 bytes and 244 at 512. Both are below the 326 to 381 of the old rows, but these came from 128 partitions at a time and the new pieces from 32, and no run here separates the two.
- **`mixed_up`: the wait was right, its size was not.** The add of `s4` does wait for POOL (until 708.17 us), but for 9.10 us of three sums, where the prediction had one operation of 2.32. The last low part was held up by the first of them; the wait of 2.55 us came from that, and the fall of the clock followed it. Pair 3 came out at -4.1 us where -6.5 was summed.

No rival came true as it was written. Nearest is the last one, a lag in pair 0 or at the hand-over: there is a lag in pair 0, but of 9 us and not of tens, its reason (new areas that wait for old tiles) is not shown, and the other loss lies at the `k` loads of pair 2, 70 us behind the hand-over.
